# New order of all engine queues in a gated linear attention and maxout kernel, planned with longer durations and later results

## The chip, the cores and the metric

The kernel runs on one core of a Trainium2 chip. The metric is the device time of one execution in microseconds (us). Each core has TensorE (PE; its weight loads are listed as PEld), VectorE (DVE), ScalarE (ACT), GpSimd (POOL) and SyncE (SP), which here only issues DMAs. Each engine works through its own queue of instructions in order, and waits on semaphores for the results of the others.

## The reference

```python
f = 1.0 / (1.0 + np.exp(-f_logit))
for t in range(S):
    state = f[:, :, t, :, None] * state + np.einsum('bhd,bhe->bhde', k[:, :, t], v[:, :, t])
    y[:, :, t] = np.einsum('bhd,bhde->bhe', q[:, :, t], state)
...
h1 = x @ w1
h2 = x @ w2
g = np.maximum(h1, h2)
return (g @ w_out)
```

q, k, v and f_logit are 4 x 8 x 768 x 48 float32 (batch, heads, time, head dimension). x is y with the heads side by side, 3072 x 384; w1 and w2 are 384 x 1024, w_out is 1024 x 384.

## The kernel before

**Samples.** The 768 times of a batch are cut into three windows of 256, so there are 12 samples s (window s // 4, batch s % 4), and sample s needs the state that sample s - 4 left. Inside a sample the 256 times lie on 128 partitions, two to each, and are worked as two half chunks.

**Steps.** All work is cut into named steps, each a small function. For a sample s:
- Lf, Lk, Lq, Lv: the DMA loads of f_logit, k, q, v (384 KB each) into one of 16 slots in SBUF (L115). Wa, Wb, Wo are the weight loads (768 KB each; L125, L129), through the same slots
- E, F, G (ACT; L246, L250, L254): exponentials and logarithm of the gate; e (L257): sum over the pair of times; C (PE; L261, L264): running sum of the logarithms; X, Z (ACT; L271, L276): exponentials of it, for k and for q
- i, j (L280, L284): k and q with the gate of the odd time; K, Q (L291, L294): padded bf16 kp and qp; V (L104, three copies): padded vb
- t, u (PE; L320): transposes of kp and qp; U (L104): their copy from PSUM into trs
- A0, A1 (PE; L337): the products of q and k; m (DVE; L345): masking into at_m; S (PE; L367): q on the state; z (DVE; L377): a look at a PSUM column; y (PE; L387): at_m on V
- D (PE; L401): kp on V, the addition to the state; n (DVE; L413, L415) and N (L418): the new state
- H (L104) and Y (DVE; L433): the output into xT

For the maxout part, max(h1, h2) is computed as h2 + relu(h1 - h2): wd = w1 - w2 in a permuted row order, m2 = w2 times w_out. d0 to d3 (PE; L445) are the products of xT and wd, r0 and r1 (L452, L454) the relu into gT, o0 and o1 (PE; L460 with m2, L463 with wo) the two output halves, b0 and b1 (L104) their copies from PSUM into ob, O (L481) the stores. The last sample's second half is cut once more: P (L491, L494), B (L104), R (L502, one store on SP and one on ACT). The weights are prepared by ws (L536), wp (L544), we, wc, wt (L512), wx, wo, wm (L528) and wn.

**What sets the order.** ORDER (L20 to L56) is a text that holds all 557 steps. A word such as `U0v@0` says: step U of sample 0, on DVE (a is ACT, v DVE, p POOL, s SP), in PSUM bank 0. L584 to L586 call the steps in this order, and the instructions of each engine stand in its queue in the order in which they were called; nothing is reordered afterwards. There are 8 PSUM banks, and a step that writes a bank waits until the step that read its former content is done. Likewise a load waits in SP's queue until its slot has been read, and all loads and stores behind it wait too. Buffers in SBUF rotate: two of gate, ell, one, inv, gT, at_m and tail, three of trs, ob, kp and qp, four of vb and xT, six of dec.

```python
    def copy(e, out, in_):
        (nc.scalar.copy if e == "a" else engines[e].tensor_copy)(out, in_)
...
    for word in ORDER.split():
        key, of, e, b = re.fullmatch(r"([A-Za-z]+)([0-9.]+)([avps]?)@?([0-9]*)", word).groups()
        steps[key](*map(int, of.split(".")), e, int(b or 0))
```

Of the kernel before, what the change touches and what calls it, by code (L numbers as in the profile page):

```python
# [12 lines left out]
BF16 = mybir.dt.bfloat16  # L13
# [4 lines left out]


ORDER = """  # L20
Lf0s@12 Lk0s@13 Lq0s@14 Lv0s@15 E0a Wb0s F0a Lf1s@12 G0a i0v Wb1s e0v C0@0 Wa0s X0a Wa1s Z0a K0v
V0p j0v t0@0 Lq1s@13 D0@2 Q0v Lv1s@15 n0.0v u0@0 E1a n0.1v U0v@0 F1a e1p A0.0@0 wc1a A0.1@2
m0.0v@0 S0@4 G1a Lk1s@12 wc0a C1@6 z0v@4 wt1@7 ws1v wc2a m0.1v@2 wp1@0 wx1a@7 ws3v y0 Z1a Wo0s
ws0v we1a@0 wp3@2 H0a@4 ws2v wt2@7 we3a@2 Wo1s wp0@0 j1v X1a wp2@2 Y0v@4 Q1p we0a@0 Lf2s@0 wt0@6
wx2a@7 we2v@2 d0.0@0 d0.1@1 i1v V1a K1v d0.2@2 Lf4s@13 r0.0a@0 u1@4 wx0v@6 t1@4 wo1p d0.3@3 U1v@4
wo0p D1@0 r0.1a@2 Lq2s@9 n1.0v A1.0@6 A1.1@4 wo3a wo2v S1@2 n1.1v Lk2s@10 m1.0v@6 wm0@0 E2a z1v@2
m1.1v@4 Lv2s@11 wm2@1 F2a E4a e2p y1 Lk4s@0 F4a C2@4 H1v@2 wm1@5 Y1v@2 Z2a e4p G2a Lq4s@13 wn0a@0
C4@6 X2a d1.0@2 i2v wn2a@1 j2v wn1a@5 d1.1@3 Lf3s@8 Z4a Q2v d1.2@0 X4a G4a K2v d1.3@1 V2a Lf5s@9
u2@4 t2@4 r1.1a@0 i4v o0.0@6 U2v@4 K4p Lv4s@11 r1.0a@2 j4v A2.0@0 b0.0a@6 Lq3s@10 D2@2 N1.1p
o0.1@4 n2.0v E3a m2.0v@0 Q4p Lv3s@0 F3a n2.1v S2@0 b0.1a@4 A2.1@2 z2v@0 E5a t4@6 N0.1p m2.1v@2  # L30
Lk3s@13 u4@6 N2.1p o1.0@5 F5a U4v@6 V4a Lf6s@9 e5v G5a y2 j3v b1.0a@5 D4@2 A4.0@6 H2a@0 O0s n4.0v
o1.1@5 m4.0v@6 N4.0p Lk5s@11 V3a e3p Lv5s@8 n4.1v G3a Y2v@0 C5@6 b1.1a@5 C3@7 i3p X5a S4@2 Z3a
A4.1@4 Lq5s@0 z4v@2 d2.0@0 Z5a Q3v X3a d2.1@1 E6a K3v d2.2@6 r2.0a@0 m4.1v@4 d2.3@7 Lq6s@13 t3@0
r2.1a@6 u3@0 i5p y4 D3@4 U3a@0 Lk6s@9 H4v@2 K5p o2.0@6 n3.0v Y4v@2 Lf8s@10 F6a n3.1v S3@0 b2.0v@6
A3.0@2 e6p A3.1@4 m3.0v@2 d4.0@6 Lf7s@11 N4.1p d4.1@7 j5v V5p d4.2@2 z3v@0 r4.0a@6 Lk8s@12 m3.1v@4
d4.3@3 G6a D5@6 Q5v r4.1a@2 y3 O1s C6@5 j6v H3a@0 o2.1@4 Lv6s@0 Z6a i6v E8a Y3v@0 Lq8s@8 X6a F8a
t5@2 N3.1v u5@2 b2.1v@4 Lv7s@10 d3.0@0 U5a@2 e8v d3.1@1 n5.0v Q6v d3.2@4 K6v E7a d3.3@5 Lq7s@13
C8@2 N5.0v r3.1a@4 o4.0@3 r3.0v@0 V6p F7a Lf10s@9 n5.1v G8a e7v N5.1p D6@0 Z8a A5.0@4 b4.0v@3 X8a
t6@6 Lf9s@0 j8v u6@6 C7@2 U6a@6 n6.0v o3.0@3 m5.0v@4 N6.0p Lk7s@11 V7p n6.1v X7a i8v A5.1@0
b3.0a@3 A6.0@6 S5@4 Lf11s@10 j7v Z7a K8p o3.1@3 z5v@4 m5.1v@0 Lq9s@15 m6.0v@6 y5 S6@0 Q8v H5a@4  # L40
Lv8s@12 A6.1@6 G7a o4.1@2 E9a z6v@0 i7p m6.1v@6 F9a Y5v@4 b3.1a@3 y6 e9p E10a O3s t8@6 u8@6 K7p
H6a@0 d5.0@3 Lk9s@9 U8v@6 G9a Lq10s@0 b4.1a@2 C9@5 d5.1@4 X9a O4s Y6v@0 Z9a N6.1p d5.2@6 r5.0a@3
O2s d5.3@7 Q7v d6.0@0 r5.1a@6 Lk11s@11 j9v A8.0@2 Lq11s@13 Q9p D7@4 V8a m8.0v@2 u7@6 t7@6 d6.1@1
U7a@6 n7.0v Lv9s@12 d6.2@2 N7.0v n7.1v d6.3@3 j10v E11a o5.0@4 r6.0v@0 r6.1a@2 N7.1v A7.0@0
Lv11s@10 b5.0a@4 D8@2 A7.1@6 F11a n8.0v S7@4 m7.0v@0 o6.0@3 F10a e11p Lk10s@15 G10a z7v@4 N8.0p
m7.1v@6 e10p C11@0 Lv10s@8 b6.0a@3 S8@1 i9v A8.1@6 V9p o5.1@3 z8v@1 m8.1v@6 K9v C10@6 y7 Z10a
b5.1v@3 D9@7 j11v H7a@4 y8 O5s Z11a Y7v@4 o6.1@3 X11a Q11p H8a@1 n9.0v Y8v@1 d7.0@4 b6.1a@3 i10p
G11a d7.1@5 O6s i11v d8.0@0 r7.0a@4 Q10v d8.1@1 N9.0v X10a d8.2@2 V10a K10v d8.3@3 r8.0a@0 K11v
d7.2@4 d7.3@5 r8.1v@2 u10@6 r7.1a@4 t9@0 u9@0 t10@6 t11@2 U9a@0 U10v@6 u11@2 o8.0@4 U11v@2 A9.0@0
b8.0a@4 S9@2 m9.0v@0 A9.1@6 D10@4 o7.1@5 z9v@2 m9.1v@6 V11v A11.0@0 y9 n10.0v D11@6 o7.0@4 n11.0v  # L50
m11.0v@0 N11.0p H9v@2 o8.1@0 b7.0v@4 N10.0v b7.1a@5 Y9v@2 O7s A10.0@6 b8.1a@0 S10@4 m10.0v@6
A10.1@2 d9.0@0 z10v@4 d9.1@1 m10.1v@2 d9.2@6 r9.0a@0 d9.3@7 A11.1@0 r9.1a@6 S11@2 y10 z11v@2
m11.1v@0 o9.0@6 H10a@4 Y10v@4 y11 b9.0a@6 d10.0@0 H11v@2 d10.1@1 d10.2@4 r10.0v@0 o9.1@6 Y11v@2
d10.3@5 d11.0@0 r10.1a@4 d11.1@1 b9.1a@6 d11.2@2 O9s d11.3@3 O8s o10.0@4 r11.1v@2 r11.0v@0 o10.1@3
o11.0@0 b10.0a@4 b10.1a@3 O10s P11.0@1 b11.0a@0 O11s P11.1@0 B11.0v@1 R11.0s B11.1a@0 R11.1s
"""  # L56


@with_exitstack
def kernel(  # L60
# [31 lines left out]
    work = ctx.enter_context(tc.tile_pool(name="work", bufs=2))  # L92
# [8 lines left out]
    engines = {"a": nc.scalar, "v": nc.vector, "p": nc.gpsimd, "s": nc.sync}  # L101
# [6 lines left out]
    slots = inp.tile([C, 22, H * 2 * D], F32, name="slots")  # L108
    loaded = {s: {} for s in range(n_s)}
    sources = {"f": f_logit, "k": k, "q": q, "v": v}  # L110

    def load(nm, s, slot):
        w, b = divmod(s, B)
        src = sources[nm][b, :, w * W:(w + 1) * W, :].rearrange("h (p two) d -> p h (two d)", two=2)
        nc.sync.dma_start(out=slots[:, slot, :].rearrange("p (h x) -> p h x", h=H), in_=src)  # L115
        loaded[s][nm] = slots[:, slot, :].rearrange("p (h two d) -> p h two d", h=H, two=2)

    def staged(i, a):
        return slots[:, 4 * i:4 * i + 4, :].rearrange("p s x -> p (s x)").rearrange("p (a x) -> p a x", a=a)
# [24 lines left out]
    for h in range(2):  # L144
        rows = slice(h * HC, (h + 1) * HC)
# [178 lines left out]
    def step_U(s, e, b):  # L324
        t = work.tile([C, 2, 2, NP, 2, HC], BF16, name="trs", tag="trs", bufs=3)
        copy(e, t.rearrange("p h x j a t -> p h (x j a t)"), banks16[:, b:b + 2, :])
        tr[s] = t

    def step_A(s, jj, b):
        t = tr[s]  # L330
        for j in range(2 * jj, 2 * jj + 2):
            for par in range(2):
                for h in range(2):
                    for r in range(2):
                        rows = slice(r * DP, r * DP + D)
                        ps = banks[:, b + r, :].rearrange("p (j a t) -> p j a t", j=2, a=2)
                        nc.tensor.matmul(out=ps[h * HC:(h + 1) * HC, j % 2, par, :],  # L337
                                         lhsT=t[rows, h, 0, j, par, :],
                                         rhs=t[rows, h, 1, j].rearrange("p a t -> p (a t)"),
                                         start=True, stop=True, skip_group_check=True)  # L340
# [16 lines left out]
    def step_S(s, b):  # L357
        t = tr[s]
        ys[s] = [banks[:, b + h, :].rearrange("p (j t) -> p j t", j=NP) for h in range(2)]
        for h in range(2):  # L360
            if not has_state(s, h):
                continue
            st = state_before(s, h)
            for j in range(NP):
                for r in range(2):
                    rows = slice(r * DP, r * DP + D)
                    nc.tensor.matmul(  # L367
                        out=ys[s][h][r * DP:(r + 1) * DP, j, :], lhsT=st[rows, j, :],
                        rhs=t[rows, h, 1, j].rearrange("p a t -> p (a t)"),
                        start=(j == 0), stop=False, skip_group_check=True)  # L370


# [176 lines left out]
    def store_wd(part, e, b):  # L549
# [67 lines left out]
```

## Time and profile before

| | |
|---|---|
| timed runs, us | 141.36, 141.38, 141.94 (median 141.38) |
| the profiled execution, its own time | 142.99 us |
| its span from first to last instruction | 141.2 us |
| granted TensorE clock | 1.000 |
| bytes moved by DMA | 28.66 MB, 203 GB/s over the span |
| SP's loads, issue to landing (L115) | 3.6 / 6.0 / 11.3 us (least, median, most) |
| SP's stores, issue to landing (L481) | 2.1 / 3.4 / 6.3 us |

In the busy table, each digit is the busy tenth of one of 40 slices of the span (3.53 us each). A line of the waits reads: engine and line that waited, the engine and line it waited for, then the sum in us, how often, and the longest. A line of the timeline reads: start, length, engine, line, operation, operands, and in brackets the idle time before it with what ended it. For a group of instructions in the timeline the length covers all of them. The ends of matmuls are modelled.

### The profile page before, as it was taken

The page shows a single profiled execution, that of the slowest core. Times are in us where ns is not written, and L with a number is a line of the kernel's source. Part 1 is how long each engine was busy: PE and PEld are TensorE (multiplying, and loading weights), DVE is VectorE, ACT ScalarE, POOL GpSimd, SP SyncE. Part 2 cuts the span into 40 slices and gives each one's busy share as a digit, 9 for nine tenths or more (in the row PEclk, how much of TensorE's full clock was granted, in tenths as well). Part 3 has the DMA queues.
Part 4 walks back from the last instruction along what each step waited for, and adds up shares of the span by engine and source line. Part 5 has one row for each costly group of instructions (what it writes and reads, how often), then busy time and mean ns, then how long its engine had stood idle before and what let it go on. Part 6 is the DMA issues. An engine that isn't in the chain of part 4 may idle for free.

```text
span 141.2 us, 5372 instructions
## 1 busy us (share of the span) xinstructions
PE 120.8 (86%) x2331; PEld 89.9 (64%) x2331; DVE 110.4 (78%) x196; ACT 87.2 (62%) x145; POOL 47.7 (34%) x68
## 2 busy tenths in 40 slices
PE   0033899896999999999699999997999999999990
PEld 0022678653866786868466787675886668678570
DVE  5766799896879997999989898899688895770610
ACT  3624899559988899499683999715785114303120
POOL 7443205405194536800582943459100000000000
PEclk9999999999999999999999999999999999999999
DMA  4999999999999998997999999999410012000854
GB/s 114 269 331 348 382 278 300 341 236 265 264 262 269 278 276 212 248 230 185 272 265 250 233 256 271 271 271 238 101 25 5 5 34 77 5 0 16 214 125 98
DMA packets 56248, 28.66 MB, mean 203 GB/s; under 512 B 50464, under 2 KB 54688, under 8 KB 56224
## 3 DMA queue, kind: packets, MB, share of 16 engines
q1 hardware_dynamic: 56064, 28.22, 80.9%
q8 instruction: 18, 0.29, 0.9%
q10 hardware_dynamic: 160, 0.10, 0.3%
q14 instruction: 6, 0.05, 0.1%
HBM read 23.59 MB, written 4.72 MB: 200 GB/s over the span
## 4 chain that ended last, share of the span: by engine, by line
PE 57%; DMA 20%; DVE 7%; issue 5%; ACT 4%; POOL 3%; SPq 1%; ACTq 0%; DVEq 0%; POOLq 0%
PE banks L445 17%; PE banks L463 17%; DMA slots<-in_f_logit_dram 8%; PE banks L460 7%; DMA slots<-in_k_dram 6%; DMA slots<-in_moe_w_dram 6%; PE banks L337 3%; PE banks L320 3%; PE banks L387 3%; PE banks L367 2%; DVE kp L291 2%; POOL vb L104 2%; PE banks L401 2%; ACT gate L246 1%; POOL wo L104 1%
## 5 line engine op out<-in xcount | busy, mean ns | idle before, releaser
L445 PE MATMUL banks<-xT,wd 128*128 128x256 bf16 x288 | 33.7, 273 | 0.0
L463 PE MATMUL banks<-wo,gT 128*128 128x384 bf16 x184 | 33.7, 326 | 0.0
L345 DVE TENSOR_TENSOR at_m<-banks,mask 128x1024 bf16<-128x1024 f32 x24 | 29.0, 1215 | 1.7 <-PE banks L337 1.2
L445 PEld LDWEIGHTS <-wd 128*128 128x128 bf16 x288 | 27.3, 98 | 3.9
L452 ACT ACTIVATE gT<-banks 128x1024 bf16<-128x1024 f32 x18 | 18.4, 1032 | 11.8 <-PE banks L445 11.6
L463 PEld LDWEIGHTS <-gT 128*128 128x128 bf16 x184 | 18.0, 98 | 11.9
L104 ACT COPY ob<-banks 128x384 f32<-128x384 f32 (+1 forms) x19 | 8.9, 468 | 19.9 <-PE banks L463 14.8
L433 DVE SCALAR_TENSOR_TENSOR xT<-tail,gaps,banks 128x256 bf16<-128x256 bf16 x36 | 15.1, 472 | 0.1
L460 PE MATMUL banks<-m,xT 128*128 128x384 bf16 x69 | 15.1, 328 | 0.0
L246 ACT ACTIVATE gate<-slots 128x768 f32<-128x768 f32 x12 | 10.1, 846 | 7.2 <-DMA slots<-in_f_logit_dram 7.2
L104 POOL CAST vb<-slots 128x384 bf16<-128x384 f32 (+2 forms) x15 | 9.3, 657 | 13.8 <-DVE gT L454 8.3
L257 POOL TENSOR_TENSOR e<-ell 128x384 bf16<-128x384 f32 x8 | 8.0, 1001 | 13.5 <-ACT ell L250 13.5
L418 POOL TENSOR_TENSOR state<-tmp_s,dec 128x256 bf16<-128x256 f32 x10 | 6.5, 651 | 17.9 <-DVE tmp_s L413 17.9
L337 PE MATMUL banks<-trs 48*64 48x128 bf16 x384 | 10.5, 227 | 1.9 <-DVE trs L104 1.9
L261 PE MATMUL banks<-e,u_inc 128*128 128x384 bf16 x12 | 4.3, 354 | 9.2 <-DVE e L257 7.8
L454 DVE TENSOR_SCALAR gT<-banks 128x1024 bf16<-128x1024 f32 x6 | 7.2, 1218 | 4.3 <-PE banks L445 4.3
L337 PEld LDWEIGHTS <-trs 48*64 48x64 bf16 x384 | 7.5, 110 | 4.5 <-DVE trs L104 2.2
L104 ACT COPY trs<-banks 128x2048 bf16<-128x2048 bf16 x5 | 9.3, 1861 | 1.6 <-PE banks L320 1.6
L250 ACT ACTIVATE ell<-gate 128x768 f32<-128x768 f32 x12 | 10.0, 844 | 0.4
L294 POOL TENSOR_TENSOR qp<-slots,dec 128x768 bf16<-128x768 f32 x4 | 7.3, 1819 | 8.7 <-DVE slots L284 6.8
L104 DVE COPY trs<-banks 128x2048 bf16<-128x2048 bf16 x7 | 8.4, 1217 | 1.5 <-PE banks L320 1.5
L291 DVE TENSOR_TENSOR kp<-slots,inv 128x768 bf16<-128x768 f32 x8 | 7.5, 952 | 1.4 <-ACT inv L271 1.2
(73 smaller groups left out, 195.3 us busy)
## 6 DMA issues: line engine op xcount, KB each, us to landing
slots<-in_f_logit_dram SPq DMA_DIRECT2D x12, 384.0 KB, 6.4
slots<-in_k_dram SPq DMA_DIRECT2D x12, 384.0 KB, 5.7
slots<-in_q_dram SPq DMA_DIRECT2D x12, 384.0 KB, 6.0
slots<-in_v_dram SPq DMA_DIRECT2D x12, 384.0 KB, 5.9
out_dram<-ob SPq DMA_DIRECT2D x22, 192.0 KB, 3.5
slots<-in_moe_w_dram SPq DMA_DIRECT2D x4, 768.0 KB, 8.4
slots<-in_moe_w_out_dram SPq DMA_DIRECT2D x2, 768.0 KB, 7.4
out_dram<-ob SPq DMA_DIRECT2D x2, 96.0 KB, 2.2
```

Of the source, the lines that this page charges most:

```text
L104: (nc.scalar.copy if e == "a" else engines[e].tensor_copy)(out, in_)
L246: nc.scalar.activation(flat(gate[s]), flat(loaded[s]["f"]), AF.Exp, bias=0.0, scale=-1.0)
L250: nc.scalar.activation(flat(ell[s]), flat(gate[s]), AF.Ln, bias=1.0, scale=1.0)
L257: engines[e].tensor_add(pad("e", s)[:, :, 0:D], ell[s][:, :, 0, :], ell[s][:, :, 1, :])
L291: engines[e].tensor_mul(pad("kp", s)[:, :, :, 0:D], by_parity(loaded[s]["k"]), both(inv[s]))
L337: nc.tensor.matmul(out=ps[h * HC:(h + 1) * HC, j % 2, par, :], lhsT=t[rows, h, 0, j, par, :], rhs=t[rows, h, 1, j].rearrange("p a t -> p ( ...
L345: nc.vector.tensor_mul(at[s][:, jj].rearrange("p r j a t -> p (r j) (a t)"), banks[:, b:b + 2, :].rearrange("p r (j x) -> p (r j) x", j=2) ...
L433: engines[e].scalar_tensor_tensor(out=x[:, kt], in0=tails[s], scalar=gaps[:, kt:kt + 1], in1=ps[:, :, kt], op0=ALU.mult, op1=ALU.add)
L445: nc.tensor.matmul(out=ps[:, f, :], lhsT=wd[:, kt, ff * C:(ff + 1) * C], rhs=xT[g][:, kt, :], start=(kt == 0), stop=(kt == KT - 1))
L452: nc.scalar.activation(dst, src, AF.Relu)
L460: nc.tensor.matmul(out=ps, lhsT=xT[g][:, kt, cols], rhs=m2[:, kt, :], start=(kt == 0), stop=False)
L463: nc.tensor.matmul(out=ps, lhsT=gT[g][:, ff, cols], rhs=wo[:, ff, :], start=False, stop=(ff == FG - 1))
```

## The change

The text ORDER is replaced by another one. It has the same 557 steps, and each step does the same work on buffers of the same number and size; what differs is the place of each step in the order, for some steps the engine, and the PSUM bank or SBUF slot. The plan behind the new order assumed durations on the long side, and that an engine sees the results of others later.

The engines that change, in numbers of steps before and after: U on ACT 5 to 3 and on DVE 7 to 9; V on ACT 6 to 8, POOL 5 to 1, DVE 1 to 3; K and Q on DVE 8 to 6 each and on POOL 4 to 6 each; e on POOL 8 to 6 and DVE 4 to 6; i on POOL 4 to 7 and DVE 8 to 5; N on POOL 10 to 11 and DVE 6 to 5; b on ACT 18 to 12 and DVE 5 to 11; wc on ACT 3 to 1 and DVE none to 2; ws on DVE 4 to 3 and POOL none to 1; we on ACT 3 to 4 and DVE 1 to none; wo on ACT 1 to 3, POOL 2 to 1, DVE 1 to none.

The first lines, two stretches from the middle, and the last lines, before (-) and after (+):

```diff
-Lf0s@12 Lk0s@13 Lq0s@14 Lv0s@15 E0a Wb0s F0a Lf1s@12 G0a i0v Wb1s e0v C0@0 Wa0s X0a Wa1s Z0a K0v
-V0p j0v t0@0 Lq1s@13 D0@2 Q0v Lv1s@15 n0.0v u0@0 E1a n0.1v U0v@0 F1a e1p A0.0@0 wc1a A0.1@2
-m0.0v@0 S0@4 G1a Lk1s@12 wc0a C1@6 z0v@4 wt1@7 ws1v wc2a m0.1v@2 wp1@0 wx1a@7 ws3v y0 Z1a Wo0s
-ws0v we1a@0 wp3@2 H0a@4 ws2v wt2@7 we3a@2 Wo1s wp0@0 j1v X1a wp2@2 Y0v@4 Q1p we0a@0 Lf2s@0 wt0@6
-wx2a@7 we2v@2 d0.0@0 d0.1@1 i1v V1a K1v d0.2@2 Lf4s@13 r0.0a@0 u1@4 wx0v@6 t1@4 wo1p d0.3@3 U1v@4
-wo0p D1@0 r0.1a@2 Lq2s@9 n1.0v A1.0@6 A1.1@4 wo3a wo2v S1@2 n1.1v Lk2s@10 m1.0v@6 wm0@0 E2a z1v@2
-m1.1v@4 Lv2s@11 wm2@1 F2a E4a e2p y1 Lk4s@0 F4a C2@4 H1v@2 wm1@5 Y1v@2 Z2a e4p G2a Lq4s@13 wn0a@0
...
+Lf0s@12 Lv0s@13 Lk0s@14 Lq0s@15 E0a Wb1s F0a Wa1s G0a e0v Lf1s@12 V0a C0@0 i0v X0a Z0a Wb0s K0v
+Wa0s j0v t0@0 Q0v D0@2 Lk1s@14 n0.0v u0@0 n0.1v U0v@0 A0.0@0 ws3v ws2p A0.1@2 Lv1s@15 S0@4 wp3@6
+z0v@4 m0.0v@0 E1a F1a Lq1s@12 m0.1v@2 wp2@0 wc1a e1v wc0v y0 we2a@0 wc2v C1@3 we3a@6 wt1@0 ws0v
+wt0@1 Lf2s@13 X1a Z1a ws1v wp0@6 H0a@4 G1a Y0v@4 wp1@2 Wo0s we0a@6 i1p we1a@2 wt2@7 V1v d0.0@5
+Wo1s wx2a@7 K1v d0.1@6 j1v D1@2 r0.0a@5 Lf4s@14 Q1v wx1v@0 E2a u1@4 t1@4 d0.2@6 wx0a@1 U1v@4
+Lk2s@13 F2a n1.0v A1.0@0 A1.1@4 n1.1v wo1a d0.3@7 m1.0v@0 e2p wo0a S1@2 N0.1p z1v@2 C2@0 r0.1a@6
+m1.1v@4 Lq2s@9 N1.1p wo2a wo3p y1 Lv2s@8 wm2@1 H1a@2 Z2a Y1v@2 E4a Lq4s@11 wm0@7 G2a wn2a@1 i2v
...
+m6.0v@6 Lf10s@8 A5.1@0 N6.1p b3.0a@5 S5@2 G7a C8@4 j8v o3.1@5 X8a z5v@2 m5.1v@0 V8a K8p Z8a y5 E9a
+S6@0 i7p H5a@2 A6.1@6 z6v@0 F9a o4.1@4 m6.1v@6 K7p b3.1a@5 E11a O3s Y5v@2 D8@7 Lv7s@15 y6 Lq10s@13
...
+b6.0v@2 Lk11s@8 j11v S8@0 b6.1a@6 e10v y7 z8v@0 i9v A8.1@6 H7a@4 o5.1@2 K9p m8.1v@6 b5.0a@3 Y7v@4
+C10@7 b5.1a@2 y8 j10v O5s D9@2 H8a@0 C11@6 n9.0v Z10a d7.0@4 O6s Y8v@0 G11a Q10p d7.1@5 X10a G10a
...
-d10.3@5 d11.0@0 r10.1a@4 d11.1@1 b9.1a@6 d11.2@2 O9s d11.3@3 O8s o10.0@4 r11.1v@2 r11.0v@0 o10.1@3
-o11.0@0 b10.0a@4 b10.1a@3 O10s P11.0@1 b11.0a@0 O11s P11.1@0 B11.0v@1 R11.0s B11.1a@0 R11.1s
+d10.3@1 d11.0@6 r10.1a@0 d11.1@7 d11.2@4 r11.0v@6 d11.3@5 o10.0@0 r11.1v@4 o11.0@7 o10.1@6
+b11.0v@7 b10.0v@0 O11s O9s P11.0@7 b10.1v@6 O10s P11.1@6 B11.0v@7 R11.0s B11.1a@6 R11.1s
```

Besides, the loop over the words becomes a function, a load names its issuing engine (s, SP, in all of them), FIRST can hold loads that are issued ahead of all else and is empty, and a step T (a transposing DMA) is defined and stands nowhere in ORDER. trs is seen through another view of the same bytes:

```diff
-        nc.sync.dma_start(out=slots[:, slot, :].rearrange("p (h x) -> p h x", h=H), in_=src)
+        engines[e].dma_start(out=slots[:, slot, :].rearrange("p (h x) -> p h x", h=H), in_=src)
...
-        tr[s] = t
+        tr[s] = t.rearrange("p h x j a t -> p x h j a t")
...
-                                         lhsT=t[rows, h, 0, j, par, :],
-                                         rhs=t[rows, h, 1, j].rearrange("p a t -> p (a t)"),
+                                         lhsT=t[rows, 0, h, j, par, :],
+                                         rhs=t[rows, 1, h, j],
```

## The prediction

> **What bounds the kernel now.** I read the busy table by slices first, then TensorE's (PE's) own waits, then the timeline around each of them, then the last microseconds.
>
> ```profile
> PE 120.8 (86%) x2331; PEld 89.9 (64%) x2331; DVE 110.4 (78%) x196; ACT 87.2 (62%) x145; POOL 47.7 (34%) x68
> PE   0033899896999999999699999997999999999990
> DVE  5766799896879997999989898899688895770610
> DMA  4999999999999998997999999999410012000854
> ```
>
> PE is full from about 20 us to 137 us; DMA is full from 4 to 99 us; DVE runs at nine tenths between. So only PE's holes can be won, besides what lies after PE's last matmul.
>
> ```profile
> PE banks L261 <- DVE e L257: 7.8, 1, 7.8
> PE banks L401 <- POOL vb L104: 3.4, 3, 1.4
> PE banks L337 <- DVE trs L104: 1.9, 2, 1.6
> PE banks L320 <- DVE kp L291: 1.9, 2, 1.6
> PE banks L261 <- POOL e L257: 1.4, 1, 1.4
> ```
>
> With some 0.1 us more these are 16.6 us, the rest being work: 120.8 + 16.6 + the end = 141.2. 14.5 us of them lie before 33.4 us. Two are later, and they are the only ones for over 100 us:
>
> ```profile
> 69.50 0.44 PE L401 MATMUL banks<-vb,kp 64*64 64x64 bf16 x32 [1.24 <-POOL vb L104]
> 96.48 0.35 PE L401 MATMUL banks<-vb,kp 64*64 64x64 bf16 x11 [0.83 <-POOL vb L104]
> ```
>
> These are D6 and D9: each waits for POOL's three casts of V, 2.0 us together (877 + 566 + 528 ns). At the end, the sync queue (SP):
>
> ```profile
> 129.20 8.25 SPq L481 DMA_DIRECT2D out_dram<-ob  x8
> 137.55 1.19 SPq L502 DMA_DIRECT2D out_dram<-ob  x2
> ```
>
> The reader is to see that SP issues one after another there, some 0.65 us each, past PE's last matmul (its modelled end is 137.54).
>
> **What the change adds up to.** The 557 steps are the same; only place, engine and PSUM bank differ. Counting engine letters and multiplying by mean durations by form: DVE gains 1.6 us and POOL 2.2, with the two prices named below (K and Q together go from 8 to 12 on POOL at 1.86 and 1.82 us, V from 5 to 1), ACT loses 3.7 us (six copies of ob at 476 ns and two of trs at 1861 ns go to DVE). ACT has slack, so the sums alone are worth nothing; the holes decide. I therefore follow the new queues with the old durations: each step starts when its engine is free, its inputs are done and its bank is empty, with 0.05 us between engines.
>
> **The start.** Landings are taken by place in the SP queue from the old transfers: 4.4, 5.9, 7.4, 8.9 us for the first four tiles, then about 2.05 us for a weight half and 1.45 us for a tile; the twelfth transfer landed at 23.96 us, and I take that.
>
> | us | before | after, worked out |
> |---|---|---|
> | e0 done | 7.74 | 6.7 (e0 goes ahead of i0 on DVE, F0 ends 6.12) |
> | K0 done | 9.87 | 9.0 (X0 ends 8.05 behind V0 on ACT; + 0.96) |
> | U0 done | 14.69 | 12.75 (D0's V is on ACT, done 7.6; POOL ended it at 11.87) |
> | m0.1 done | 18.72 | 16.7 (ws3 waits for Wa1, 13.0; then 0.15 + 2 x 1.15) |
> | d0.0 starts | 22.83 | 21.7 (Wa0 lands 18.55, ws0 0.95, wp0 0.8, we0 0.8) |
> | u1, t1 start | 24.92, 25.66 | 25.8, 26.1 (Lq1 now last, 23.96; K1, j1 0.56, Q1 0.95) |
> | m1.1 done | 31.48 | 30.75 |
> | d1.3 done | 37.97 | 38.1, with C4 (0.27) still to do |
>
> So the 2 us won early are lost again: before, wm0 and wm2 (2.7 us) ran ahead of y1, while data came; now they stand behind y1, and PE waits some 1.3 us for K1, 0.9 for Q1, 0.55 for U1 and 0.9 for m1.1. The front ends **0.4 us later**. Ends of the range: -0.8 if Lq1 lands 1.45 us behind its predecessors all along (in the trace one tile behind the weights took 2.66 us), +1.0 if three DVE steps there are stretched, as priced next.
>
> POOL beside DVE is one row to weigh: DVE's L280, about 555 ns alone, took up to 911 ns while POOL worked; L284, about 550, up to 900; K and Q (L291, L294) stayed at 941 to 962 either way. The longer POOL steps K and Q thus cost at most 0.36 us per meeting with an i or j. The Trainium skill ("GPSIMD Engine Reference", Specifications) says POOL shares its SBUF interfaces with VectorE and contends with every VectorE instruction that has two SBUF inputs. That speaks against this change; by it alone K and Q on DVE would be stretched too, and the middle would be 1 us or more worse, an estimate; this trace shows no such stretch for them.
>
> Two operations have no row. ws2 on POOL (128x768 subtract): between 0.95 us (the same on DVE) and 1.86 (a multiply of that size on POOL); I take 1.86, done 14.9 us, while its bank comes free at 15.6: nothing either way. wc on DVE (128x1024 cast): between 0.56 us (768 columns on DVE) and 1.04 (ACT, same size); I take 0.75; it ends before the bank that wt0 also waits for: nothing, at most 0.3.
>
> **The middle.** From there I carry PE forward by its work. V6 goes to ACT: Lv6 lands about 64 us (E7 ends 59.7 and frees its slot, + 3.65, the time of the first load), V6 is done at 65.5, D6 comes up at 69.7. V9 also goes to ACT: about 91 us against D9 at 97.4. Both holes close: **-2.1 us** (between -2.1 and 0; the nearest rows are the holes themselves). What is late next is DVE between 70 and 80 us: n6.1 ends 72.2 for A5.1 at 72.4, m5.1 ends 75.2 for y5 at 75.3, Y5 ends 78.9 for d5.0 at 79.4. With j8 stretched by 0.36 these turn into waits: **+0.7** (0.3 to 1.1, two to three such stretches).
>
> **The end.** Before, O9 and O8 were issued at 129.2 to 131.8, ahead of O10. Now O9 stands behind O11, both of them ready long before or at once. With E the end of PE: o11.0 ends E-3.6, b11.0 (DVE, 0.55) E-3.0; then O11 twice 0.54, O9 twice 0.65, O10 twice 0.65, R11.0 0.65: R11.1 goes out at E+1.35; before it was E+0.65 (138.19). **+0.7** (0 to 0.8). The skill ("DMA: Bandwidth & Descriptors", Issuing engines are not separate DMA queues) calls the issuing time usually small relative to the DMA itself; by it this term would be near 0 and the time 140.4. Here an issue took 0.65 us against about 2.0 to landing, ten in a row, so I go by the row.
>
> **Sum.** +0.4 - 2.1 + 0.7 + 0.7 = -0.3 us. The profiled execution's span was 141.2 (its own time 142.99, profiler included); the median of the three timed runs is 141.38, 0.2 above the span. I take the difference to the median: **141.1 us**, its own range 139.9 (front at -0.8) to 142.2 (front +1.0, DVE +1.1).
>
> **Rivals.**
> 1. *Slower: the sync queue stalls on O3 and E11.* In SP's queue Lv7 now stands directly behind O3; O3 waits for b3.1 (o3.1 ends about 75.3, then H5, F9, b3.1 on ACT: 77.4), Lv7 for E11 (78.3), which frees its slot. By then all earlier loads have landed (about 75.1), so DMA runs dry for 3 us. Ten transfers follow before Lk9, at 1.45 each: 94 to 95 us. i9 (0.6) and then K9, now on POOL (1.86), must end before D9 at 97.4. Each microsecond of Lk9 past 95 delays D9 one for one. For: before, the loads issued between 50 and 75 us took 5.1 to 7.0 us to land, and the 1.45 us allow no wait for a slot. Against: my sum just meets it. Two late: 141.1 + 1.8 = 142.9.
> 2. *Faster: the front's early gain survives.* Lq1 lands early (-0.8) and the DVE stretches are few (+0.3): -0.8 - 2.1 + 0.3 + 0.7 = -1.9, 139.5. For: PE has 1.9 us in hand at U0. Against: every transfer in that place is bound by a full DMA.
> 3. *The spacing does nothing: waits move, they do not go.* Other late results take the place of D6's and D9's 2.1 us; the rest stays: +0.4 + 0.7, 142.5. For: DVE is at nine tenths, so a different order meets a full engine. Against: by work alone DVE is done with m7.1 9.7 us ahead of y7, before 6.7.
>
> **Chances.** Forecast 0.42, first rival 0.28, second 0.18, third 0.12. A measurement of this kernel tells about 0.5% (0.7 us) from no change. Faster (under 140.67): 0.16 of the second rival and a quarter of the forecast's, 0.27. Slower (over 142.09): 0.26 of the first, 0.10 of the third, 0.02 of the forecast's, 0.38. Within: 0.35. The range 139.4 to 143.2 leaves out half the second rival and a quarter of the first.
>
> **What would show it.** Right: L401 no longer waits for POOL's vb; PE's holes before 32 us are at d0 to y1, not at C2; L502's issues on SP start 0.7 us later after PE's end. Wrong: PE waits over 1 us for kp from POOL near 97 us, or SP's waits for ob or gate near 77 us over 4 us followed by PE waits (first rival); new PE waits on DVE spread over 45 to 95 us (third); PE's holes before 38 us below 14 us (second).

## The result, and the profile after

The changed kernel takes 146.95 us (median of 4 runs, 145.99 to 147.63), the kernel before, beside it on the same chip, 141.66 (median of 4, 141.36 to 142.54). The ratio is 1.036 (95% interval 1.028 to 1.044): 5.3 us slower, where 0.3 us faster was forecast, and 3.75 us past the upper end of the range. Ratios, here and below, leave out runs more than 1.5% above the fastest of their kernel; medians and ranges include them.

The profiled execution of the changed kernel took 146.66 us of its own, with a span of 144.9. From the page, the busy times and the slices that were read of before:

```profile
PE 123.1 (85%) x2331; PEld 89.6 (62%) x2331; DVE 115.1 (79%) x203; ACT 83.2 (57%) x144; POOL 51.9 (36%) x62
...
PE   0136958589999999979999998999999999999950
...
DVE  5787959878898989999995983899996798866220
...
DMA  4999999999999999999972599999800401200074
```

DVE is busy 4.7 us longer than before, where the shift of its steps was to add 1.6. DMA, which held full to 99 us, now has a dent in slices 21 to 23 (72 to 83 us). TensorE's waits, longest first, with the two casts of V that this was to settle:

```profile
PE banks L273 <- DVE e L269: 6.8, 1, 6.8
PE banks L359 <- DVE trs L113: 2.4, 2, 1.4
PE banks L332 <- DVE kp L303: 1.9, 1, 1.9
PE banks L566 <- DVE wdn L558: 1.5, 1, 1.5
PE banks L332 <- DVE qp L306: 1.3, 2, 0.9
PE banks L409 <- DVE at_m L367: 1.2, 2, 0.7
PE banks L359 <- ACT gT L474: 0.5, 1, 0.5
```

(Lines after the first hundred stand 9 to 22 lower in the changed file: D is L423, A L359, y L409, m L367, K L303, Q L306, i L292, j L296, N L440, e L269, O L503, R L524, loads L124, copies L113.) The wait of D for POOL's vb is gone from the list, and D6 and D9 start without a hole. New after 50 us are waits for at_m (m is DVE's masking) and gT. And the end of SP's queue:

```profile
136.74 3.98 SPq L503 DMA_DIRECT2D out_dram<-ob  x6
140.81 1.35 SPq L524 DMA_DIRECT2D out_dram<-ob  x2
```

Six stores of ob stand ahead of R now, and the last R is issued at 141.47, 1.75 us after PE's modelled end (139.71); before it was 0.65 after.

**Where the time came from.** I cut each execution at two steps that both orders have: the start of u2, with the 0.27 us of C4 added for the changed order, which still has C4 to do there ("front"), and the start of P11.1 ("middle" up to it, "tail" from it to the last instruction). Later runs gave a second profile of each unchanged kernel; all four stand here. "DVE extra" is the sum, over DVE's steps that ran beside a POOL step, of the time above what the same form takes undisturbed.

| us | own time | front | middle | tail | DVE extra |
|---|---|---|---|---|---|
| before | 142.99 | 37.97 | 98.50 | 4.74 | 1.7 |
| before, second profile | 141.24 | 37.45 | 97.26 | 4.75 | 1.6 |
| after | 146.66 | 38.71 | 99.93 | 6.24 | 4.5 |
| after, second profile | 147.2 | 38.81 | 100.34 | 6.27 | 3.6 |

The first profile of before, on which the prediction stood, was a long execution: 142.99 of its own against a median of 141.4 to 142.3 in the four sets of timed runs. Against it the changed kernel lost 0.74 + 1.43 + 1.50 = 3.7 us; against the second profile 1.26 + 2.67 + 1.49 = 5.4, which is what the timed medians show (5.3). All three parts lost. The loss in front is the least certain: with the two later runs that keep the order of before up to u2 (b_before_v 38.12, c_before2 37.76) the fronts of before lie between 37.45 and 38.12, and the nine profiles with the order of after, c_x6 aside, between 38.67 and 39.02; their medians are 0.9 us apart.

### The profile page after: what moved, and what is told of

Same layout as the page of the kernel before. It is cut to its first block, busy times and chain, and to the rows that moved or that the text cites. A ratio compares the mean times of both kernels' runs of the same rounds, so it can differ in the third digit from the quotient of the medians.

```text
span 144.9 us, 5368 instructions
## 1 busy us (share of the span) xinstructions
PE 123.1 (85%) x2331; PEld 89.6 (62%) x2331; DVE 115.1 (79%) x203; ACT 83.2 (57%) x144; POOL 51.9 (36%) x62
## 4 chain that ended last, share of the span: by engine, by line
PE 57%; DMA 13%; DVE 12%; ACT 9%; issue 3%; SPq 2%; ACTq 0%; DVEq 0%
PE banks L467 16%; PE banks L485 15%; DMA slots<-in_moe_w_dram 7%; PE banks L482 6%; DVE at_m L367 4%; PE banks L359 3%; PE banks L409 3%; DMA slots<-in_v_dram 3%; PE banks L550 3%; DMA slots<-in_f_logit_dram 3%; PE banks L332 2%; PE banks L389 2%; DVE kp L303 2%; ACT gate L258 2%; SPq L137 2%
## 5 line engine op out<-in xcount | busy, mean ns | idle before, releaser
L467 PE MATMUL banks<-xT,wd 128*128 128x256 bf16 x288 | 34.5, 273 | 0.3 <-DVE trs L113 0.3
L367 DVE TENSOR_TENSOR at_m<-banks,mask 128x1024 bf16<-128x1024 f32 x24 | 29.0, 1217 | 2.2 <-PE banks L359 2.1
L474 ACT ACTIVATE gT<-banks 128x1024 bf16<-128x1024 f32 x18 | 18.3, 1023 | 8.8 <-PE banks L467 8.5
L113 ACT COPY ob<-banks 128x384 f32<-128x384 f32 (+1 forms) x13 | 6.1, 466 | 17.1 <-PE banks L516 8.9
L303 POOL TENSOR_TENSOR kp<-slots,inv 128x768 bf16<-128x768 f32 x6 | 11.0, 1830 | 8.1 <-ACT gT L474 3.1
L292 POOL TENSOR_TENSOR slots<-slots,one 128x384 f32<-128x384 f32 x7 | 7.0, 1006 | 16.6 <-ACT one L266 10.8
L440 POOL TENSOR_TENSOR state<-tmp_s,dec 128x256 bf16<-128x256 f32 x11 | 9.0, 819 | 9.6 <-DVE tmp_s L435 9.6
L359 PE MATMUL banks<-trs 48*64 48x128 bf16 x384 | 9.8, 227 | 2.9 <-DVE trs L113 2.4
L113 DVE COPY trs<-banks 128x2048 bf16<-128x2048 bf16 x9 | 10.9, 1219 | 1.5 <-PE banks L332 1.5
L306 POOL TENSOR_TENSOR qp<-slots,dec 128x768 bf16<-128x768 f32 x6 | 10.9, 1816 | 1.7 <-ACT dec L288 1.7
L359 PEld LDWEIGHTS <-trs 48*64 48x64 bf16 x384 | 7.3, 111 | 5.9 <-DVE trs L113 2.8
L113 ACT CAST vb<-slots 128x384 bf16<-128x384 f32 (+2 forms) x24 | 8.1, 407 | 4.2 <-DMA slots<-in_v_dram 4.2
L296 DVE SCALAR_TENSOR_TENSOR slots<-gate,slots 128x384 f32<-128x384 f32 x12 | 8.3, 688 | 2.3 <-DMA slots<-in_q_dram 2.2
L409 PE MATMUL banks<-at_m,vb 64*64 64x128 bf16 x384 | 8.7, 219 | 1.3 <-DVE at_m L367 1.2
```

Source lines behind the costliest of these rows:

```text
L303: engines[e].tensor_mul(pad("kp", s)[:, :, :, 0:D], by_parity(loaded[s]["k"]), both(inv[s]))
L306: engines[e].tensor_mul(pad("qp", s)[:, :, :, 0:D], by_parity(loaded[s]["q"]), both(dec[s][:, 0:HD].rearrange("p (h d) -> p h d", h=H)))
L409: nc.tensor.matmul(out=ys[s][h][r * DP:(r + 1) * DP, j, :], lhsT=vb[rows, 2 * j + r, par, :], rhs=m[rows, j // 2, r, j % 2, par, :], start ...
L467: nc.tensor.matmul(out=ps[:, f, :], lhsT=wd[:, kt, ff * C:(ff + 1) * C], rhs=xT[g][:, kt, :], start=(kt == 0), stop=(kt == KT - 1))
L474: nc.scalar.activation(dst, src, AF.Relu)
```

## The experiments

### Two engines on one lock

In the middle of the changed kernel, DVE's timeline from 55 to 62 us (start, length, and so on) reads

```profile
55.52 1.36 DVE L296 SCALAR_TENSOR_TENSOR slots<-gate,slots 128x384 f32<-128x384 f32 x1
56.80 1.21 DVE L367 TENSOR_TENSOR at_m<-banks,mask 128x1024 bf16<-128x1024 f32 x1
57.93 0.54 DVE L296 SCALAR_TENSOR_TENSOR slots<-gate,slots 128x384 f32<-128x384 f32 x1
58.40 0.95 DVE L306 TENSOR_TENSOR qp<-slots,dec 128x768 bf16<-128x768 f32 x1
59.27 2.57 DVE L303 TENSOR_TENSOR kp<-slots,inv 128x768 bf16<-128x768 f32 x1
```

and POOL's in the same stretch

```profile
55.46 1.00 POOL L292 TENSOR_TENSOR slots<-slots,one 128x384 f32<-128x384 f32 x1 [1.87 <-ACT one L266]
56.42 0.93 POOL L440 TENSOR_TENSOR state<-tmp_s,dec 128x256 bf16<-128x256 f32 x1
59.13 1.89 POOL L303 TENSOR_TENSOR kp<-slots,inv 128x768 bf16<-128x768 f32 x1 [1.78 <-issue]
```

The same step j (L296) takes 1.36 us when POOL started i5 60 ns earlier, and 0.54 when POOL rests. K5 on DVE takes 2.57 instead of 0.95: it starts 0.14 us behind POOL's K6 and ends 0.81 after K6 ends (61.02), almost its whole own length later. So the second one does not run at half speed; it stands until the first is done. Behind K5 in DVE's queue stand z3 and m3.1, and PE's y3 and, behind it, D5 wait for those:

```profile
61.61 0.76 PE L409 MATMUL banks<-at_m,vb 64*64 64x128 bf16 x16
63.09 0.42 PE L409 MATMUL banks<-at_m,vb 64*64 64x128 bf16 x16 [0.72 <-DVE at_m L367]
```

N5.0 behind POOL's e7 is the third: 1.08 us instead of 0.42.

**bench** measures this by itself. It leaves the kernel's computation out: DVE does six steps and POOL three, alone and together, in 13 phases on tiles in SBUF and PSUM.

> This kernel leaves out the whole computation: it runs VectorE and GpSimd steps on 128x768 float32 tiles, alone and side by side. Theory A (an exclusive lock: when both engines run an instruction with two SBUF inputs, the second waits until the first has ended): side by side, six VectorE multiplies of 953 ns and three GpSimd multiplies of 1820 ns take about the sum of both, near 11 us, against 5.5 us for the longer alone; VectorE's casts with one SBUF input, and its multiplies and copies that read PSUM, are not stretched. Theory B (what the prediction took from the rows: a stretch of at most 0.36 us per meeting, none for a 768 wide multiply): the pair takes 5.5 to 6.5 us and single VectorE instructions at most 1.3 us.

Measured, from its timeline; a line covers the six or three steps of a phase. DVE first: two SBUF inputs alone, a cast alone, a product with PSUM alone, then two inputs beside POOL's two inputs (33.44), a cast beside them (64.34), and a product and a cast from PSUM beside them (78.73 and 82.31):

```profile
4.93 5.30 DVE L42 TENSOR_TENSOR dv<-in,b 128x768 bf16<-128x768 f32 x6 [2.04 <-ACT in L67]
22.05 2.90 DVE L48 CAST dv<-in 128x768 bf16<-128x768 f32 x6 [11.82 <-ACT in L67]
24.87 3.67 DVE L51 TENSOR_TENSOR dv<-banks,mask 128x512 bf16<-128x512 f32 x6
...
33.44 10.12 DVE L42 TENSOR_TENSOR dv<-in,b 128x768 bf16<-128x768 f32 x6 [1.31 <-ACT in L67]
...
64.34 7.72 DVE L48 CAST dv<-in 128x768 bf16<-128x768 f32 x6 [1.96 <-ACT in L67]
...
78.73 3.67 DVE L51 TENSOR_TENSOR dv<-banks,mask 128x512 bf16<-128x512 f32 x6
82.31 3.67 DVE L54 CAST dv<-banks 128x512 bf16<-128x512 f32 x6
```

POOL, alone and beside the three:

```profile
11.65 5.32 POOL L57 TENSOR_TENSOR po<-in,b 128x768 bf16<-128x768 f32 x3 [11.20 <-ACT in L67]
...
33.55 7.45 POOL L57 TENSOR_TENSOR po<-in,b 128x768 bf16<-128x768 f32 x3 [12.81 <-ACT in L67]
...
64.45 6.25 POOL L57 TENSOR_TENSOR po<-in,b 128x768 bf16<-128x768 f32 x3 [4.62 <-ACT in L67]
...
80.88 5.32 POOL L57 TENSOR_TENSOR po<-in,b 128x768 bf16<-128x768 f32 x3 [3.42 <-ACT in L67]
```

5.30 and 5.32 us of work take 10.12 together: nearly one after the other (10.62), not side by side. DVE's cast, which reads one SBUF tile only, pays the same: 2.90 becomes 7.72 (2.90 + 5.32 = 8.22). So does a cast on POOL: it took DVE's two-input steps to 7.18 and DVE's casts to 4.78. With an operand in PSUM, DVE's 3.67 stays 3.67 (a cast from PSUM took 3.67 alone, too) and POOL's 5.32 stays 5.32; POOL started at 80.88, so the last 1.5 us of the products and all of the casts ran beside it. What follows, for the forms run here: DVE and POOL take turns as long as DVE's operands are all in SBUF, casts included, and a meeting costs the one that comes second what is left of the other's instruction, not the 0.36 us I had read off.

The Trainium skill has this rule, on a page that the prediction did not draw on: "SBUF — State Buffer", in the section on SBUF's two separate sides, says that DVE and GpSimd share a pair of ports under an exclusive lock held for the whole instruction, and that it is taken by DVE instructions with two SBUF inputs and by those in a fast two-port mode, which it names for fp32 copies. The bench agrees. Its casts, from fp32 to bf16, would then be of the second kind: they take 0.48 us each for 768 columns, against 0.88 for two inputs, but no run here shows the mode itself.

**a_lock** takes away the three meetings by moving POOL's three steps to DVE:

```diff
-i5p ... K6p ... e7p
+i5v ... K6v ... e7v
```

> The changed kernel with K6, i5 and e7 moved from GpSimd to VectorE, the order as it is. Theory A (three VectorE steps, j5, K5 and N5, stood still for 0.8, 1.6 and 0.7 us because GpSimd's i5, K6 and e7 held the shared SBUF access): K5 takes 0.96 us again, the holes of TensorE at S3, y3 and d3.1 to d3.2 shrink from 2.65 us to under 1, and the last matmul ends 1.2 to 2 us sooner than 139.7, although VectorE has 2.1 us more to do. Rival B (VectorE is simply too full between 50 and 70 us in the new order): the extra work delays y3 and d3 further, and the end comes 1 to 2 us later.

Measured: 148.34 us (146.91 to 148.74), ratio 1.045 (1.035 to 1.055); middle 102.09, so 2.2 us worse than after. j5, K5 and N5.0 were back at 0.55, 0.95 and 0.42. But with K6 gone from its queue, POOL came to Q6 earlier and met DVE's next step with it. DVE's line is for K5 and K6 together (0.95 and 2.57 us):

```profile
59.64 3.44 DVE L303 TENSOR_TENSOR kp<-slots,inv 128x768 bf16<-128x768 f32 x2
```

and POOL's is

```profile
59.62 2.64 POOL L306 TENSOR_TENSOR qp<-slots,dec 128x768 bf16<-128x768 f32 x1 [4.61 <-ACT dec L288]
```

What follows: the lock's price moved along to the next pair, and DVE had 3 steps more. By its time alone the run came out as rival B said; K6's 1.62 us over its usual length is the lock's, and the two are not told apart. The run doesn't tell what the lock costs; it shows that a POOL step is not simply taken away from beside DVE.

**b_free** keeps the engines and shifts two steps in order: G5 on ACT behind r2.1, which makes POOL's i5 start behind j5, and K5 on DVE behind m3.1, so that the wait no longer stands ahead of m3.1.

```diff
-... G5a ... K5v ... m3.1v@0 ... r2.1a@0
+... r2.1a@0 G5a ... m3.1v@0 K5v
```

> The changed kernel with two steps moved, engines and work unchanged: G5 behind r2.1 on ScalarE (so that GpSimd's i5 starts after VectorE's j5), and K5 behind m3.1 on VectorE (so that GpSimd's K6 runs while VectorE works from PSUM). Theory A (the lock between VectorE and GpSimd, by chance at j5 and K5): j5 takes 0.55 and K5 under 1.4 us; y3 starts within 0.3 us of d4.3's end; D5 starts at 61.7 to 62.2 instead of 63.3; but Lv7, late because SyncE's queue waits for O3 and E11, then stops TensorE at D7 for 2 to 3 us, so that the last matmul comes only 0 to 0.8 us sooner than 139.7. Rival B (VectorE too full): y3 and D5 stay where they were.

Measured: 145.91 us (145.70 to 146.19), ratio 1.026 (1.022 to 1.031), so about 1 point of the 3.6 back, though the two intervals overlap. DVE extra fell from 4.5 to 2.4 us, with new meetings of 0.4 to 0.6 us at Q5, j6, K5, N5.0. So the lock was eased, not gone: D5 started at 62.58 instead of 63.31 (61.7 to 62.2 was expected), yet P11.1 only 0.3 us earlier: the next section says why.

### Lv7 behind O3 in the sync queue

SP's timeline in the changed kernel shows where the dent in DMA comes from. Behind Lf10, at 72.55 us, nothing was issued until 79.81; there SP waited with O3 for ob:

```profile
79.81 1.26 SPq L503 DMA_DIRECT2D out_dram<-ob  x2
81.56 0.38 SPq L124 DMA_DIRECT2D slots<-in_v_dram  x1
```

Lv7 behind it landed at 85.80, V7 on ACT waited for it, and so did D7; a relu of d (r, L474) stands behind V7 in ACT's queue, and A8.0 waited 0.47 us for its gT:

```profile
85.82 1.02 ACT L113 CAST vb<-slots 128x384 bf16<-128x384 f32 x3 [1.74 <-DMA slots<-in_v_dram]
...
87.81 0.42 PE L359 MATMUL banks<-trs 48*64 48x128 bf16 x16 [0.47 <-ACT gT L474]
```

That is the first rival's mechanism, at D7 instead of D9.

**a_slot** puts Lv7 into slot 16, which nothing else uses, and ahead of O3:

```diff
-... Lf10s@8 ... O3s ... Lv7s@15
+... Lf10s@8 Lv7s@16 ... O3s
```

> The changed kernel with only the load Lv7 moved: into a slot that nothing else uses (16), and ahead of O3 in SyncE's queue. If SyncE's wait for O3's ob and for E11 is what makes V7 late, DMA no longer runs dry at 76 to 80 us, D7 and A8.0 come without holes, and the last matmul ends 0.6 to 0.9 us sooner (about 139.0). If not, the holes of 0.8 us at D7 and A8.0 stay.

Measured: 145.08 us (144.29 to 146.70), ratio 1.023 (1.016 to 1.031). Lv7 landed at 81.33, and D7 and A8.0 had no hole. But middle fell by 2.6 us to 97.32, more than the 0.8 us of holes and more than expected. The rest is the lock, which fell the other way in this execution, without any edit there. DVE's j5 and K5:

```profile
55.67 0.55 DVE L296 SCALAR_TENSOR_TENSOR slots<-gate,slots 128x384 f32<-128x384 f32 x1
...
59.09 0.95 DVE L303 TENSOR_TENSOR kp<-slots,inv 128x768 bf16<-128x768 f32 x1
```

and POOL's i5 and K6, which now are the second and the stretched ones:

```profile
55.73 1.34 POOL L292 TENSOR_TENSOR slots<-slots,one 128x384 f32<-128x384 f32 x1 [1.87 <-ACT one L266]
...
59.42 2.29 POOL L303 TENSOR_TENSOR kp<-slots,inv 128x768 bf16<-128x768 f32 x1 [1.77 <-issue]
```

j5 started 60 ns ahead of i5 here, 60 ns behind it in the profile of after. Those 0.1 us decide whether DVE stands for 0.8 us or POOL for 0.3, and with j5 done early K5 is ahead of K6 as well. (Below 0.1 us the starts in a profile don't tell who comes first: in a_tail j5 started 20 ns behind i5 and was not stretched, i5 was, to 1.43 us.) So a_slot alone can't price Lv7; **b_free_slot**, both edits at once, beside b_free on the same chip, can:

> The former kernel with Lv7 also in a slot of its own ahead of O3. Theory A: lock and SyncE stall are both gone; the last matmul starts at 136.0 to 136.6 and the span is 142.3 to 142.7, as in the run with the slot alone, in which the lock happened not to strike; and the runs scatter less. Rival B: 1 to 2 us later than that.

Measured: 144.40 us (143.50 to 145.00), ratio 1.015 (1.008 to 1.022), against 145.91 for b_free: 1.5 us for Lv7, and 1.7 between the middles (99.59 to 97.87). Against the expectation the lock was not gone in this execution: DVE extra was 3.7 us, with Q5 stretched by 0.8 and K5 by 1.0, and the runs scattered more than those of b_free, not less. What follows: the stall of SP costs 1.5 to 1.7 us with the moves of b_free, though the profile of after shows 0.8 us of holes for it, because the delay at y3 and D5 lay in front of the same wait for Lv7. The clearest sight of it is the next run, a_tail, which had no lock to speak of (DVE extra 0.6) but Lv7 in its old place:

```profile
PE banks L423 <- ACT vb L113: 2.4, 1, 2.4
```

There the stretch from t7 to A8.0 took 7.18 us, in a_slot 4.04: 3.1 us for Lv7.

Five profiles have the meetings at j5 and K5 with the order of after, and fell differently. TensorE's steps come in the same order in all of them (c_load has two copies of ob on ACT there); the times are from start to start:

| profile | K5 behind K6 | Lv7 behind O3 | d4.1 to C7 | t7 to A8.0 | d4.1 to A8.0 |
|---|---|---|---|---|---|
| after | yes | yes | 13.13 | 4.85 | 31.16 |
| after, second profile | yes | yes | 13.13 | 5.17 | 31.49 |
| c_load (two sections on) | yes | no | 13.10 | 4.04 | 30.32 |
| a_tail | no | yes | 10.91 | 7.18 | 31.67 |
| a_slot | no | no | 10.91 | 4.04 | 28.21 |

So the lock costs 2.2 us before C7. With the lock gone but Lv7 still late nothing is left of that at A8.0; with Lv7 early and the lock still there 0.8 us is won; with both gone 3.0. c_x6 (below), whose edit makes K5 come first and moves Lv7, has 10.96, 4.04 and 28.18.

### The last stores

**a_tail** moves O9 in SP's queue ahead of O11, to behind b9.1:

```diff
-... b10.0v@0 O11s O9s P11.0@7 ...
+... b9.1a@0 O9s ... b10.0v@0 O11s P11.0@7 ...
```

> The changed kernel with only O9 moved up, directly behind b9.1, as it was ready at about 125 us. If SyncE's issuing sets the end, the last store is issued 1.0 to 1.3 us sooner, and the time from the last matmul to the end falls from 5.2 us to about 3.7; span 143.4. If the transfers themselves set it, the end stays within 0.4 us.

Measured: the tail fell from 6.24 to 5.17 us, by 1.07. Whether the time did can't be told: 146.56 us (145.25 to 148.16), ratio 1.033 (1.021 to 1.044). The profiled execution had no gain, since D7's wait took more than that in it. **b_all** adds the same move to b_free_slot:

> The former with O9 up behind b9.1. The span falls by another 1.0 us, to 141.3 to 141.7, on a level with the kernel before: the terms that were found are then all there is, but for the front, 0.7 us later, and what the closed holes at D6 and D9 give. If the time stays 1.5% over the kernel before, something is still missing in the account.

Measured: 143.97 us (142.98 to 144.33), ratio 1.012 (1.006 to 1.018); tail 5.21 instead of 6.13, span 141.85 (141.3 to 141.7 was expected), timed 0.4 us less than b_free_slot, within both ranges. SP's end in b_all, two stores fewer than in after:

```profile
134.73 3.08 SPq L503 DMA_DIRECT2D out_dram<-ob  x4
137.91 1.45 SPq L524 DMA_DIRECT2D out_dram<-ob  x2
```

So the three edits, which touch four of the 557 steps, bring 1.036 down to 1.012.

### What is left

Two runs tried to get further from there, both with Lv7 and O9 moved. **c_x6** moves X6, Z6 and K6 behind E7 (instead of the two moves of b_free), so that POOL's K6 meets no step of DVE. **c_load** takes four copies of ob (b0.0, b2.0, b4.0, b6.0) from DVE to ACT.

> The changed kernel with Lv7 in its own slot ahead of O3 and O9 up behind b9.1, and, against the lock, only X6 and Z6 moved behind E7 on ScalarE, so that GpSimd's K6 starts about 0.9 us later, after VectorE's K5 has begun. Theory A: K5 takes 0.96 us as in the two runs in which it happened to come first; D5 starts near 61.9, the last matmul at 136.1 to 136.6, and with the tail of 5.2 us the span is 141.2 to 141.8; the timed runs come within 1% of each other, at a median of 142.8 to 143.5. Rival B (VectorE's load): no better than 144.0.

> The changed kernel with the same two moves of DMAs (Lv7, O9), and four copies of ob (b0.0, b2.0, b4.0, b6.0) moved from VectorE to ScalarE; K6 and K5 as they were. Rival B (VectorE is too full between 45 and 95 us): 2.2 us less work on it make TensorE's holes at y3 and d3.1 to d3.2 close, and the runs come at 142.5 to 143. Theory A: the holes depend on whether GpSimd's K6 starts ahead of VectorE's K5; where it does, K5 still takes 2.5 us; the runs scatter between 143 and 145.5, as with Lv7 alone less 1 us.

Measured: c_x6 144.35 us (143.95 to 145.63), ratio 1.017 (1.012 to 1.021); c_load 144.22 (144.10 to 145.82), 1.017 (1.012 to 1.022). Neither beats b_all, nor is either shown to be worse, as the intervals overlap. Both expectations named faster times for theory A (c_x6) or B (c_load). In c_load K5 met K6 again (2.57 us; middle 98.50): four copies fewer on DVE did not keep them apart. In c_x6 DVE extra is down to 0.9 us and the middle to 97.13, as short as in the second profile of before (97.26). What its profile lost lies in the front, 40.12 us instead of 38.8, and one line of the windows says where it ran otherwise (the 0.57 is the granted clock):

```profile
28.00:32.00 4.00, 3.72 (x67) 2.55 (x68) 2.86 (x6) 2.87 (x5) 2.26 (x4) 0.57 1.01 268
```

In the profile of b_all the clock of this stretch is 1.00, and the six matmuls of d0.3 start 0.76 us ahead of the next step instead of 1.39. It does not explain the timed runs: two of the other three had a granted clock of 1.000 over the whole execution, so no such stretch, and took 144.48 and 143.95. What holds c_x6 there stays open; its time is the one that rival B named.

**b_before_v** and **c_before2** go from the other end: the kernel before, with one of the change's ideas alone. In b_before_v V6 and V9 go to ACT (V6 behind F7). In c_before2 only V9 does, and Lv6 goes into the unused slot 16, directly behind Lf7, so that it need not wait for a slot.

```diff
-V6p ... V9p
+V6a ... V9a
```

```diff
-... Lf7s@11 ... Lv6s@0 ... V9p
+... Lf7s@11 Lv6s@16 ... V9a
```

> The kernel before with only V6 and V9 moved from GpSimd to ScalarE (V6 behind F7). This is the part of the change that the prediction counted as gain. If the holes of TensorE at D6 and D9 are GpSimd's slow casts, they fall from 2.07 us to under 0.9 (V6 still waits for Lv6, 67.9) and the time by about 1.2 us (0.8%). If the data are late anyway, the time stays.

> The kernel before with V9 on ScalarE, and Lv6 in slot 16, which nothing else uses, ahead of Lk8 in SyncE's queue; V6 stays on GpSimd. If the holes at D6 and D9 are late V6 and V9, both go: 2.0 us less, 139.4 against 141.4. If V6's casts on GpSimd, now at 64.5 to 66, meet K6 and Q6 on VectorE, part of it is lost again: 140 to 140.8.

Measured: b_before_v 141.55 us (10 runs, 141.03 to 141.98) against 142.04, ratio 0.996 (0.993 to 0.999): D9's hole is closed, D6 still waits 0.7 us, for ACT's vb. c_before2 141.11 us (6 runs, 140.38 to 141.51) against 142.32 (11 runs, 141.65 to 144.10), ratio 0.992 (0.988 to 0.995): 0.8% faster than the kernel before. The holes were thus real, but worth 0.5 to 1.2 us, half of what was expected, not 2.1 us.

**d_before** and **d_after** profile the two unchanged kernels once more, to see what of the 1.4 us between profiles and timed runs is a matter of the single execution.

> The kernel before, once more. If its first profile was a longer execution than most, this one has a span of 139.3 to 140.2 us, and the step at which it leaves the first profile is where that one lost 1.0 to 1.9 us; the two holes at D6 and D9 (1.24 and 0.83 us) stand as they did. If the first profile was an ordinary one and own time and timed runs differ by something outside the span, the span is 141.0 to 141.4 again.

> The changed kernel, once more. If the lock theory is right, what varies from one execution to the next is who comes first where DVE and POOL meet: K5 on DVE takes 2.56 us again where K6 on POOL starts ahead of it, and about 0.95 us where K5 starts first, then D5 starts near 62 us instead of 63.3, D7 and A8.0 wait the longer for Lv7, and the span is 144.0 to 145.5 either way. If the stretches come from something fixed (the instructions themselves being dearer in the new places), K5 takes 2.5 us again whoever comes first.

Measured: d_before has a span of 139.5, d_after 145.4; their rows stand in the first table. What I had expected of d_before was wrong in one point, and it is the instructive one. TensorE's wait for vb is 2.1 us in two waits, not 3.4 in three:

```profile
PE banks L261 <- DVE e L257: 8.2, 1, 8.2
PE banks L401 <- POOL vb L104: 2.1, 2, 1.4
```

The hole at D6 is not there. The lines of POOL's V6 tell why; first before, then d_before:

```profile
68.03 1.42 POOL L104 CAST vb<-slots 128x384 bf16<-128x384 f32 x3 [8.33 <-DVE gT L454]
```

```profile
66.57 1.09 POOL L104 CAST vb<-slots 128x384 bf16<-128x384 f32 x3 [7.44 <-DMA slots<-in_v_dram]
```

Lv6 was issued at 62.41 and landed at 67.91 in the first, at 61.18 and 66.45 in the second; V6 started 0.12 us after the landing in both, though the first line names another releaser. So 1.24 of the 2.07 us that the change was to win existed in the profiled execution and not in the other. In d_after K6 was first again (59.24 against 59.38) and K5 took 2.57 us, as it did in after.

The second profile of before also shows a longer stretch than the 0.36 us of the prediction. First the row that this was read from, i9 behind POOL's e10 in before; then j4 behind POOL's K4 in d_before, 0.64 us over its usual 0.55:

```profile
91.67 1.00 POOL L257 TENSOR_TENSOR e<-ell 128x384 bf16<-128x384 f32 x1
...
92.18 0.91 DVE L280 TENSOR_TENSOR slots<-slots,one 128x384 f32<-128x384 f32 x1
```

```profile
38.24 1.81 POOL L291 TENSOR_TENSOR kp<-slots,inv 128x768 bf16<-128x768 f32 x1 [3.82 <-DVE slots L280]
...
39.28 1.19 DVE L284 SCALAR_TENSOR_TENSOR slots<-gate,slots 128x384 f32<-128x384 f32 x1
```

## Why the prediction was wrong, point by point

- **The front, +0.4.** +0.74 against the profile that it was reckoned from, within its bounds (-0.8 to +1.0); +1.26 against the second, 0.9 by the medians of all fronts. Up to m0.1 the table of starts was good to 0.2 us (e0 6.76 for 6.7, U0 12.70 for 12.75, m0.1 16.71 for 16.7). Then Wa0 landed at 19.86 instead of 18.55, so d0.0 started at 23.16 instead of 21.7, and PE waited 1.5 us at wp for wdn. No run undid this; it is read off the traces only, and why Wa0 came later than reckoned stays open.
- **D6 and D9, -2.1.** Both holes closed, 2.07 us against the first profile, as worked out. But the term was a single execution's: in the second profile there was 0.76 us to win. V9 alone on ACT and an earlier Lv6 brought 1.2 us to the kernel before (c_before2).
- **DVE stretched by POOL, +0.7 (0.3 to 1.1).** This is the step that failed: "The longer POOL steps K and Q thus cost at most 0.36 us per meeting with an i or j", and none to K or Q. In after a j was stretched by 0.81, a K by 1.62 and an N by 0.66, later another j by 0.83 and an i by 0.52. On PE's side, set against a_slot, it is 0.42 us more behind A3.1, 1.23 more in y3 and 0.52 more in d3.0 and d3.1, 2.2 us in all (the 2.65 in the expectation of a_lock was too high). The 0.36 was no bound; it was what was left of POOL's e10 and N5.1 when two DVE steps happened to come up. In the second profile of before, j4 was stretched by 0.64. K and Q on DVE stood at 0.94 to 0.96 us in before because 13 of the 16 met no step of POOL and two of the other three came first. The row showed the mechanism, I took its size for its limit, and I put the rule of the Trainium skill aside on that ground; the bench's 10.12 us are on the side of the rule.
- **The sync queue.** The first rival had the mechanism and its start: O3 held SP until 79.81, DMA ran dry, and Lv7 was late. But it took Lk9 and D9 as the point that decides. D7, two samples earlier, was it: V7 moved to ACT, just as V6 and V9 did, and I had not asked when Lv7 lands. My sum had this at nothing; it was 0.8 us in the profile of after, 1.5 to 1.7 by b_free_slot against b_free.
- **The end, +0.7.** 1.49 in the profiles, of which O9's place is 1.07 (a_tail) or 0.92 (b_all). I had R11.1 at 1.35 us after PE's end; it was 1.75. Right was that SP's issues, one after another, set the end; the rest of some 0.45 us stays in b_all, which still has O11 and O10 ahead of R.
- **The base.** "[T]he median of the three timed runs is 141.38, 0.2 above the span" was no check: in each run here own time is the span and about 1.8 us, so an execution with a span of 141.2 belongs to 143.0, and the median of 141.4 to one of 139.6. The profile was 1.0 to 1.6 us longer than the median, and I subtracted holes from it that the second profile has only in part. (The upper end of the forecast's own range adds up to 142.1, not 142.2.)

In sum, against the first profile: +0.74 front, -2.07 + 2.2 + 0.8 in the middle, +1.50 at the end, 3.2 of the 3.7 us; the other 0.5 us, in the middle, I have not traced. The base adds 1.3 us (142.99 against 141.66). b_all stands 2.4 us of span above the second profile of before: 1.36 in the front, 0.57 in the middle, 0.46 at the end. So the front is the largest part that no edit here gave back (0.9 us by the medians). Of the signs named beforehand two came: SP's wait for ob near 77 us (5.9 us) with PE waits behind it, which was the first rival's, and new PE waits on DVE, here between 57 and 68 us, the third's. That the meetings at j5 and K5 cost 2.2 us is shown by profiles, in which they fell otherwise by chance or by the edit of c_x6; no timed median shows that gain by itself.

## What to carry to other kernels

Before moving work to POOL, list which of its steps will run beside DVE steps with all operands in SBUF, and price each meeting at what is left of the instruction that came first, with whatever stands behind the loser in its queue; steps with a PSUM operand are the ones to place beside POOL. A hole in one profile is a term of the sum only if own time and the timed median agree, or a second profile shows it too; and when a step moves to a faster engine, ask first when its input lands, since a load behind a waiting store comes only after it. Two delays in a row on the same path hide each other: price them with both gone, then with one.

## What the runs showed that was not expected

- 0.1 us of difference in start decides which of DVE and POOL stands still: after and a_slot have the same steps there, and K5 took 2.57 us in the one, 0.95 in the other.
- Casts lock like two-input steps: 2.90 us of DVE casts became 7.72 beside 5.32 us of POOL products.
- A stretch of c_x6 ran at a granted clock of 0.57 (28 to 32 us), and the front ended 1.3 us later than in b_all, whose clock there was 1.00 with the same steps in the same order up to that point.
